# One value buffer instead of two, a twenty-fifth resident weight quarter, and 4 KB output runs in a fused attention and soft-mixture kernel

## The chip, the cores and the metric

The kernel runs on one core of one Trainium2 chip. The metric is the device time of one execution in microseconds (us); what is quoted for a kernel is the median of its runs. A trace is one profiled execution, and its times count from the start of its span.

## What is computed

Forgetting attention over 8 batches of 8 heads, 576 positions and 64 channels, then a soft mixture of 8 experts over all 4608 tokens, in float32 (cut to what matters):

```python
scores = q @ k.T / sqrt(D) + (cum[:, None] - cum[None, :])      # cum = cumsum(log f), causal
attn = softmax(scores); x = (attn @ v) as [4608, 512]           # all heads of a token side by side
logits = x @ phi                                                # 32 slots, 4 for each expert
d = softmax(logits, axis=0); slot_in = d.T @ x                  # over all 4608 tokens: running maximum
slot_out[e] = relu(slot_in[e] @ w1[e]) @ w2[e]                  # w1 [512, 1024], w2 [1024, 512] for each expert
out = softmax(logits, axis=1) @ slot_out
```

The experts need `slot_in` of all tokens, so their two layers and the output can start only when attention has ended. The weights are 33.6 MB, the output 9.4 MB.

## The kernel before, in words

**Attention** works on pairs of heads: 32 pairs, one for each turn of the loop over `g`, with heads `h0 = 2g` and `h1 = 2g + 1`. A turn computes score tiles twice (`s1`, L219, for the row maxima that VectorE takes in `tops`, L232, one and a half pairs ahead; `s2`, L269 and L270, for the exponentials of ScalarE, `expo`, L276), lets GpSimd clear what is above the diagonal (`causal`, L284 and L287), and ends with `s3` (L302): 50 products of the probabilities with the values `V`, on TensorE 100 matmuls in the trace. The order of each engine's instructions is written out by hand; each engine runs its own in that order. `V` holds two pairs: `load_v(g + 1)` (L167) at the head of turn `g` fills the buffer that `s3(g - 1)` has just left, for the turn after.

All loads and stores are issued by SyncE (SP), in order, on one hardware queue that feeds 16 DMA engines. A turn issues, in this order: the values (325 KB), queries and keys of a later pair (`load_qk`, L163, 576 KB), one weight quarter (`wload`, L116, 512 KB) in turns 5 to 28, a row of maxima (L254), and two copies inside SBUF for a later pair (`dup_q` L192 and `dup_k` L188, 288 KB each). These two stand last, so the next turn's `V` queues behind them.

**Weights.** Each expert's two layers are cut into 8 quarters of 512 KB (1024 columns of 128 partitions), 64 in all. 24 (`NRES`) have buffers of their own (`w`) and are loaded during attention. The other 40 are streamed (`wstream`): into buffers that attention leaves (`RAW`, pools `p`, `PTS`, `V`, `XTS`, `X`) from turn 28 on, and at last into the resident buffers as the experts use them up. Quarters are used in the order first layers of all experts, first halves of the second layers, second halves.

**Tail.** After the last turn the last batch's logits give the slot maxima (`spread` L385, `mgroup` L375, `mcast` L398, `tokens` L425, `shift` L440, `shift2` L444, `dispatch` L455), then the slot inputs are turned (L870). `cols` (L683) turns the combine weights of batches n and n + 4 into `cT`. Then come the first layers (`mlp1` L898, ReLU L906 and L908), the turning of their rows into columns (`own` L918, two experts at a time, four times), the second layers (`mlp2` L928) in two halves of the output columns, and the output blocks (`block` L998, copies L1002, stores L1004). While the second halves of the second layers run, blocks of the first half are already computed and stored.

The first 5 (`FIRST`) blocks are done by halves of 256 columns: their stores go out in runs of 1 KB (20 stores of 256 KB). The last 4 blocks are done whole, in runs of 4 KB (8 stores of 512 KB).

Of the kernel before, what the change touches and what calls it, by code (L numbers as in the profile page):

```python
# [18 lines left out]
P = 128  # L19
# [9 lines left out]
NRES = 24  # L29
NQ = 8 * NE  # L30
QW = 1024
FIRST = 5
# [36 lines left out]
def attn_softmoe(ctx: ExitStack, tc: tile.TileContext, qk, v, f, phi, w1, w2, cst, out):  # L69
# [9 lines left out]
    ctok = const.tile([P, B, NBLK, NS], F32, name="ctok")  # L79
# [8 lines left out]
    mask = fr[1].tile([P, 448], F32, name="mask")  # L88
# [13 lines left out]
    V = per.tile([P, 2, NBLK, 130], F32, name="V")  # L102

    LGM = const.tile([P, 290], F32, name="LGM")
    LG, LD, TK = LGM[:, 2:146], LGM[:, 2:162].rearrange("p (t s) -> p t s", t=NBLK), LGM[:, 162:290]
# [59 lines left out]
    def load_v(g):  # L165
        if pair(g):
            nc.sync.dma_start(V[:, g % 2], v[g])  # L167

# [54 lines left out]
    def tops(i, *which):  # L223
        if not head(i):
            return
        g, h = divmod(i, 2)
        for n in which:
            bank, o, blk, j0, w = TOPS[n]
            t = st["top", i % 2, bank]
            m0 = max(448 - (128 * blk + 64) + j0, 0)  # L230
            top = MT[g % 3][:, NBLK * h + blk : NBLK * h + blk + 1] if g else m2[h][:, blk, 1:2]
            nc.vector.tensor_tensor_reduce(  # L232
                out=t[:, o : o + w], in0=t[:, o : o + w], in1=mask[:, m0 : m0 + w], scale=1.0, scalar=top if n == 3 else -3.0e38,
                op0=ALU.add, op1=ALU.max, accum_out=top,
            )
# [61 lines left out]
    def s3(g, values):  # L297

        for h, t, u, c in values:
# [3 lines left out]
                pvv[h][64 * u : 64 * u + 64, t, :], PT[h][:, at : at + 64], V[:, g % 2, c, 65 * h : 65 * h + 65], start=(c == 0), stop=(c == r // 2)  # L303
# [67 lines left out]
    def upper(b):  # L371
        if b < B - 1:
# [45 lines left out]
    def tokens(b, *ns):  # L418
# [5 lines left out]
        for n in ns:  # L424
            nc.tensor.transpose(st["tok", b][:, 128 * n : 128 * n + 128], ((LG if b < B - 1 else V.rearrange("p u t c -> p (u t c)")[:, QW:])[:, 0:128], TK)[n], ident)  # L425

    def tcopy(b):

        if batch(b):
            nc.scalar.copy(ctok[:, b], st["tok", b][:, 0 : NBLK * NS].rearrange("p (t s) -> p t s", t=NBLK))  # L430
# [4 lines left out]
    def shift(b):  # L435
# [4 lines left out]
        nc.vector.tensor_tensor(weight(b), ctok[:, b], top, op=ALU.subtract)  # L440
# [5 lines left out]
    def dispatch(b, *ts):  # L446
# [9 lines left out]
        if NBLK - 1 not in ts:  # L456
            return
# [8 lines left out]
    def combine(b, step):  # L466
# [3 lines left out]
        ce = ctok[:, b]  # L470
# [32 lines left out]
    nc.sync.dma_start(mask, cst[:, 258:706])  # L503
# [134 lines left out]
    load_v(1)  # L638
# [18 lines left out]
    nc.vector.memset(TK, 0.0)  # L657
# [9 lines left out]
    def split(b, *parts):  # L667
# [4 lines left out]
        if 0 in parts:  # L672
            nc.scalar.copy(hi, ctok[:, b::4])
        if 1 in parts:
            nc.vector.tensor_tensor(lo, ctok[:, b::4], hi.bitcast(F32), op=ALU.subtract)
# [17 lines left out]
    for g in range(1, NG):  # L693
# [3 lines left out]
        load_v(g + 1)  # L697
# [69 lines left out]
        tops(u1, 0, 1)  # L767
        s2(h1, 3, 4)
        s1(u1, 4, 5)
        mturn(g + 1)  # L770
        s2(h1, 5)
        mrows(g + 1)
# [7 lines left out]
        if g == 29:  # L780
            sides[2].close()
            p2 = fresh(ctx, "p2", 2)
            wstream(RAW[30 % 3], *p2)
        if g == 30:
# [6 lines left out]
            wstream(*p0, *p1, RAW[31 % 3])  # L791
# [28 lines left out]
        s3(g, VALUES[29:])  # L820
        if w == 0:
# [4 lines left out]
    wstream(V, PTS[:, QW : 2 * QW], PTS[:, 2 * QW : 3 * QW])  # L826
# [19 lines left out]
    srep = PTS[:, 3 * QW : 3 * QW + 128]  # L846
# [12 lines left out]
    dispatch(b - 1, 2, 3, 4)  # L859
# [7 lines left out]
    next(c0)  # L867
    next(c0)
# [6 lines left out]
    for c in (c0, c0, c1, c1, c1, c1):  # L875
        next(c)
# [8 lines left out]
    hs = V.rearrange("p u t c -> p (u t c)")[:, QW : QW + 256], XTS[:, 2 * QW : 2 * QW + 256]  # L885
# [16 lines left out]
    def relu(e):  # L902

        to, scale = hs[e // 2 % 2], mk[:, e : e + 1]
        if e % 2 == 0:
            nc.vector.tensor_scalar(to, PH[e][:, 0:256], scale, 0.0, op0=ALU.mult, op1=ALU.max)  # L906
        else:
            nc.vector.scalar_tensor_tensor(to, in0=PH[e][:, 0:256], scalar=scale, in1=to, op0=ALU.mult, op1=ALU.max)  # L908
# [23 lines left out]

    nc.vector.tensor_scalar_mul(mk, mk, fin[:, 2:3])
# [3 lines left out]
    for e, k in STEPS[:-NE]:  # L937
# [8 lines left out]
        if (e, k) in ((2, 0), (4, 0), (6, 0), (0, 4)):  # L946
            own({2: 0, 4: 2, 6: 4, 0: 6}[e])
# [4 lines left out]
        if (e, k) == (3, 0):  # L952
            combine(b, 1)
            combine(b, 2)
        if (e, k) == (7, 0):
            late.close()
# [8 lines left out]
    outv = out.rearrange("(h m p r) c -> p h m r c", h=2, p=P, r=2)  # L965
    stage = [t.rearrange("p a b -> p (a b)") for t in RAW] + p2 + p0
# [13 lines left out]
    held = [0, 0]  # L980

    def room(w):

        if held[1] + w > QW:
            held[:] = held[0] + 1, 0
        held[1] += w
        return stage[held[0] % len(stage)][:, held[1] - w : held[1]].rearrange("p (r c) -> p r c", r=2)

    def block(m, c=slice(0, DM)):

        w = c.stop - c.start
# [86 lines left out]
```

## Time and profile before

| | |
|---|---|
| median of 3 runs | 385.07 us (384.04 to 386.41) |
| profiled execution | 383.55 us, its span 381.8 us, mean granted TensorE clock 0.987 |
| TensorE (PE) busy | 360.7 us, 94% of the span |
| VectorE (DVE), ScalarE (ACT), GpSimd (POOL) | 74%, 70%, 68% |
| moved by DMA | 93.71 MB, mean 245 GB/s |
| by fortieths of the span, from the 31st on | 156 263 356 366 408 407 406 350 359 337 GB/s |

How to read it: in the first 300 us TensorE is busy nearly all the time and the DMA engines are not; in the last 80 us the DMA engines are full. `PEld` is TensorE's weight load, `SPq` the issue of a DMA by SyncE. A row of a timeline has start, duration, engine, line, operation, output and inputs, count, and in brackets the idle time before it with what ended it.

### The profile page before, as it was taken

How to read it: one execution, taken by the hardware profiler on the slowest of the kernel's cores; microseconds unless marked ns; L12 is line 12 of the kernel's file. 1: busy time of each engine (PE TensorE's matmuls, PEld its weight loads, DVE VectorE, ACT ScalarE, POOL GpSimd, SP SyncE). 2: the span in 40 equal slices, each digit the busy share in tenths (PEclk: the TensorE clock that was granted, in tenths of full speed). 3: DMA queues.
4: the chain of work that ended last, by engine and by line, in shares of the span. 5: the costliest groups of instructions: out<-in, count | busy, mean ns of one | idle time of the engine just before them, and what ended most of it. 6: DMA issues, size and time to landing. Idle time of an engine off the chain costs nothing.

```text
span 381.8 us, 15204 instructions
## 1 busy us (share of the span) xinstructions
PE 360.7 (94%) x5841; PEld 324.6 (85%) x5841; DVE 281.5 (74%) x1134; ACT 268.6 (70%) x673; POOL 261.5 (68%) x377
## 2 busy tenths in 40 slices
PE   7999999999999999999999999999999997999950
PEld 6788999999999999999999999999999985555730
DVE  7987787889788978897889788978888544421551
ACT  8869787878787878787878787878778554002740
POOL 8797888878887888788788888888788832000000
PEclk9999999999999999999999999999999999999995
DMA  7756757677868786878687767777776899999998
GB/s 216 200 154 173 185 162 208 198 230 232 251 182 237 225 252 188 243 211 258 187 244 199 243 199 237 220 217 218 220 217 156 263 356 366 408 407 406 350 359 337
DMA packets 34196, 93.71 MB, mean 245 GB/s; under 512 B 4184, under 2 KB 10126, under 8 KB 34124
## 3 DMA queue, kind: packets, MB, share of 16 engines
q1 hardware_dynamic: 34124, 92.75, 77.7%
q8 instruction: 46, 0.75, 0.8%
q14 instruction: 26, 0.21, 0.2%
HBM read 63.95 MB, written 9.73 MB: 193 GB/s over the span
## 4 chain that ended last, share of the span: by engine, by line
PE 81%; DMA 9%; DVE 3%; ACT 2%; issue 1%; POOL 1%; SPq 0%; DVEq 0%; ACTq 0%; POOLq 0%
PE pv L302 23%; PE ring L269 14%; PE ring L270 12%; PE s L219 12%; PE pv L328 4%; PE ring L898 4%; PE pv L928 2%; PE ds L455 2%; DMA YA<-YA 2%; PE ring L928 2%; PE lg L363 2%; DMA WB<-WA 1%; DMA V<-in_v 1%; DMA V<-in_w 1%; DMA out<-p 1%
## 5 line engine op out<-in xcount | busy, mean ns | idle before, releaser
L276 ACT ACTIVATE PTS<-ring 128x320 f32<-128x320 f32 (+2 forms) x256 | 118.6, 502 | 45.6 <-PE ring L270 41.5
L232 DVE CUSTOM_DVE_ANT_0 s<-s,mask 128x320 f32<-128x320 f32 (+4 forms) x320 | 138.2, 453 | 5.4 <-PE s L219 0.5
L269 PE MATMUL ring<-YA,WA 67*128 67x320 f32 (+9 forms) x384 | 121.6, 329 | 0.6 <-DMA YA<-YA 0.4
L270 PE MATMUL ring<-YB,WB 128*128 128x320 f32 (+4 forms) x384 | 110.7, 296 | 0.0
L302 PE MATMUL pv<-V,PTS 128*64 128x65 f32 x3200 | 102.2, 223 | 1.1 <-POOL PTS L284 1.0
L302 PEld LDWEIGHTS pv<-V,PTS 128*64 128x64 f32 x3200 | 97.1, 138 | 4.2 <-POOL PTS L284 1.5
L219 PE MATMUL s<-WA,YA 66*128 66x288 f32 (+9 forms) x384 | 96.8, 306 | 1.5 <-ACT WA L539 0.4
L198 POOL TENSOR_TENSOR WB<-RAW,WB 64x576 fp32r<-64x576 f32 x64 | 90.4, 1414 | 7.8 <-DMA WB<-WA 2.9
L203 POOL TENSOR_TENSOR YB<-RAW,YA 64x576 fp32r<-64x576 f32 x64 | 89.8, 1422 | 2.5
L269 PEld LDWEIGHTS ring<-YA,WA 67*128 67x128 f32 (+3 forms) x384 | 69.0, 181 | 6.3 <-issue 1.4
L270 PEld LDWEIGHTS ring<-YB,WB 128*128 128x128 f32 (+1 forms) x384 | 69.8, 182 | 0.0
L219 PEld LDWEIGHTS s<-WA,YA 66*128 66x128 f32 (+1 forms) x384 | 64.1, 190 | 5.9 <-DVE LGM L232 1.3
L232 DVE DVE_READ_ACCUMULATOR2_ANT few<- 128x1 f32 x372 | 52.8, 142 | 0.0
L287 POOL TENSOR_SCALAR_AFFINE_SELECT PTS<-PTS 128x128 f32<-128x128 f32 (+1 forms) x128 | 31.5, 267 | 27.4 <-ACT PTS L276 26.3
L172 ACT CAST WA<-RAW 64x576 fp32r<-64x576 f32 x64 | 40.2, 669 | 5.9 <-DMA RAW<-in_qk 5.2
L284 POOL TENSOR_SCALAR_AFFINE_SELECT PTS<-PTS 128x384 f32<-128x384 f32 x64 | 33.4, 523 | 12.5 <-ACT PTS L276 8.1
L177 ACT CAST YA<-RAW 64x576 fp32r<-64x576 f32 x64 | 40.3, 671 | 0.5
L232 DVE CUSTOM_DVE_ANT_0 s<-s,mask,few 128x288 f32<-128x288 f32 x62 | 32.6, 526 | 9.0
L328 PE MATMUL pv<-cs,X 128*128 128x128 f32 x156 | 37.2, 272 | 0.2 <-DVE X L321 0.2
L321 DVE TENSOR_TENSOR X<-pv,rl 128x320 f32<-128x320 f32 (+1 forms) x65 | 31.6, 487 | 2.4 <-DMA V<-in_v 0.3
L316 DVE TENSOR_SCALAR rl<-pv 128x5 f32<-128x5 f32 x64 | 10.5, 164 | 27.8 <-PE pv L302 27.4
L352 ACT COPY XTS<-pv 128x128 f32<-128x128 f32 (+1 forms) x93 | 24.9, 305 | 0.0
(198 smaller groups left out, 345.2 us busy)
## 6 DMA issues: line engine op xcount, KB each, us to landing
w<-in_w SPq DMA_DIRECT2D x45, 512.0 KB
RAW<-in_qk SPq DMA_DIRECT2D x31, 576.0 KB
V<-in_v SPq DMA_DIRECT2D x32, 325.0 KB
WB<-WA SPq DMA_DIRECT2D x31, 288.0 KB
YB<-YA SPq DMA_DIRECT2D x31, 288.0 KB
p<-in_w SPq DMA_DIRECT2D x7, 512.0 KB
out<-RAW SPq DMA_DIRECT2D x12, 256.0 KB
out<-p SPq DMA_DIRECT2D x5, 512.0 KB
```

The costliest lines, as they stand in the source:

```text
L172: nc.scalar.copy(WA[g % 3][0:64, S * h : S * h + S], RAW[g % 3][64:128, h])
L177: nc.scalar.copy(YA[g % 3][0:64, h, 64:640], RAW[g % 3][0:64, h])
L198: nc.gpsimd.tensor_tensor(t[0:64], RAW[g % 3][64:128, h], t[64:128].bitcast(F32), op=ALU.subtract)
L203: nc.gpsimd.tensor_tensor(YB[g % 2][64:128, h], RAW[g % 3][0:64, h], YA[g % 3][0:64, h, 64:640].bitcast(F32), op=ALU.subtract)
L219: nc.tensor.matmul(t[:, o : o + w], ya[0:m, h, 128 * blk : 128 * blk + 128], wa[0:m, j0 : j0 + w], start=True, stop=True)
L232: nc.vector.tensor_tensor_reduce(out=t[:, o : o + w], in0=t[:, o : o + w], in1=mask[:, m0 : m0 + w], scale=1.0, scalar=top if n == 3 else ...
L269: nc.tensor.matmul(o, wa[0:m, j0 : j0 + n], ya[0:m, h, 64 + i0 : 64 + i0 + w], start=True, stop=False)
L270: nc.tensor.matmul(o, wb[:, j0 : j0 + n], yb[:, h, i0 : i0 + w], start=False, stop=True)
L276: nc.scalar.activation(PT[i % 2][:, SEG_O[bank] : SEG_O[bank] + at], t[:, 0:at], AF.Exp, scale=0.125)
L284: nc.gpsimd.affine_select(d3, d3, pattern=[[0, 3], [1, 128]], compare_op=ALU.is_ge, fill=0.0, base=0, channel_multiplier=-1)
L302: nc.tensor.matmul(pvv[h][64 * u : 64 * u + 64, t, :], PT[h][:, at : at + 64], V[:, g % 2, c, 65 * h : 65 * h + 65], start=(c == 0), stop= ...
L328: nc.tensor.transpose(pm[:, 0:128], x[:, t, p % 2, 0:128], ident)
```

## The change

It does these things at once:

- `V` has one buffer. `load_v(g)` takes the place of `load_v(g + 1)` at the head of turn `g`; the values of pairs 30 and 31 are loaded at the end of turns 29 and 30, behind `s3`.
- The room (with a shorter mask whose zeros are read twice, `ctok` for 7 batches, and `TK` laid into `PTS`) makes a 25th resident quarter, loaded in turn 29. 39 quarters are streamed.
- The last batch: `mgroup` before `spread`, `spread` on three engines from a copy in `VF`, three steps of `dispatch(6)` ahead of `mcast`.
- `own` turns all experts' rows once, after the last first layer, with `cols` of batches 2, 6 and 3, 7 on either side of it.
- The output is laid out as [2, 9, 128, 1024], so that each half block is one store of 512 KB in 4 KB runs: 18 stores. The rows are put in order outside the device program.

```diff
-NRES = 24
+NRES = 25
-FIRST = 5
...
-    V = per.tile([P, 2, NBLK, 130], F32, name="V")
+    V = per.tile([P, NBLK, 130], F32, name="V")
+    VF = V.rearrange("p t c -> p (t c)")
...
     def load_v(g):
         if pair(g):
-            nc.sync.dma_start(V[:, g % 2], v[g])
+            nc.sync.dma_start(V, v[g])
...
+            if m0 < 0:
+                to = to.rearrange("p (a c) -> p a c", a=2)
+                by = mask[:, 0 : w // 2].rearrange("p (o c) -> p o c", o=1).broadcast_to([P, 2, w // 2])
...
-        load_v(g + 1)
+        if g < NG - 2:
+            load_v(g)
...
             p2 = fresh(ctx, "p2", 2)
-            wstream(RAW[30 % 3], *p2)
...
-            wstream(*p0, *p1, RAW[31 % 3])
+            wstream(*p0, *p1[:2])
...
         s3(g, VALUES[29:])
+        if g in (29, 30):
+            load_v(g + 1)
+            wstream(*((RAW[0], *p2) if g == 29 else (p1[2], RAW[1])))
...
     wstream(XTS[:, 0:QW])
+    mgroup(b)
     spread(b)
-    mgroup(b)
-    dispatch(b - 1, 1)
+    dispatch(b - 1, 1, 2, 3)
     mcast(b)
...
-    def own(e):
-        pm = turn()
+    def own():
+        pm = po[1]
         for c in range(2):
-            nc.tensor.transpose(pm[:, 128 * c : 128 * c + 128], hs[e // 2 % 2][:, 128 * c : 128 * c + 128], ident)
-        for n in (e, e + 1):
+            nc.tensor.transpose(pm[:, 128 * c : 128 * c + 128], hs[:, 128 * c : 128 * c + 128], ident)
+        for n in range(NE):
...
-        if (e, k) in ((2, 0), (4, 0), (6, 0), (0, 4)):
-            own({2: 0, 4: 2, 6: 4, 0: 6}[e])
...
         if (e, k) == (7, 0):
+            for _ in c2:
+                pass
+            own()
+            for _ in c3:
+                pass
...
+    def block(m, c):
+        stage.append(stage.pop(0))
+        o, pm = stage[-1], [turn() for _ in range(2)]
         for r in range(2):
...
+        for h in range(2):
+            copies[h](o[:, 512 * h : 512 * h + 512], pm[h])
+        nc.sync.dma_start(out[c, m], o)
...
     ring += [bank[0], po[0]]
-    block(0, half[0])
-    block(1, half[0])
+    block(0, 0)
     mlp2(3, 1)
+    block(1, 0)
     mlp2(4, 1)
-    block(2, half[0])
     mlp2(5, 1)
+    block(2, 0)
     mlp2(6, 1)
...
     mlp2(7, 1)
     gathered(1)
-    block(4, half[0])
+    block(3, 0)
+    block(4, 0)
```

What the diff does not tell is how the queues stand now. On SP, at the end of attention (turns 29 to 31; `RAW`, `p`, `PTS` and `w` here are weight quarters, `YA` the row of maxima, `YB` and `WB` the two copies), before:

```order
L167 DMA V<-in_v 128x650
L254 DMA YA_87<-YA_83 1x10x128
L192 DMA YB_85<-YA_83 64x2x576
L188 DMA WB_86<-WA_84 64x1152
L116 DMA RAW_93<-in_w 128x1024
L116 DMA p_0_5290<-in_w 128x1024
L116 DMA p_1_5291<-in_w 128x1024
L167 DMA V<-in_v 128x650
L254 DMA YA_83<-YA_83 1x10x128
L116 DMA p_0_5438<-in_w 128x1024
L116 DMA p_0_5442<-in_w 128x1024
L116 DMA p_1_5443<-in_w 128x1024
```

and now:

```order
L167 DMA V<-in_v 128x650
L116 DMA w_128<-in_w 128x1024
...
L192 DMA YB_85<-YA_83 64x2x576
L188 DMA WB_86<-WA_84 64x1152
L167 DMA V<-in_v 128x650
L116 DMA RAW_93<-in_w 128x1024
...
L260 DMA YA_83<-YA_83 1x10x128
L116 DMA p_0_5438<-in_w 128x1024
L116 DMA p_0_5442<-in_w 128x1024
L116 DMA p_1_5443<-in_w 128x1024
L167 DMA V<-in_v 128x650
L116 DMA p_2_5444<-in_w 128x1024
```

The first `V` row is pair 30 before and pair 29 now; the last `V` row is pair 31 in both. Before, it stood ahead of the first quarters into `p_0_5438` and its two neighbours; now it stands behind all three.

On TensorE, the last batch's chain before (L455 is `dispatch(6)` into `ring`, and `dispatch(7)` into `more`):

```order
L363 MATMUL lg_5568<-XTS,phis 32x144 x4
L455 MATMUL ring_139<-X_97,LGM 32x129 x2
L455 MATMUL ring_139<-X_98,LGM 32x129 x2
L398 MATMUL pv_138<-cs,mb_5678 128x128
L425 MATMUL more_5647<-cs,V 128x128
L425 MATMUL more_5647<-cs,LGM 128x128
```

and now, all of it up to the same place:

```order
L369 MATMUL lg_5569<-XTS,phis 32x144 x4
L467 MATMUL ring_140<-X_97,LGM 32x129 x2
L467 MATMUL ring_140<-X_98,LGM 32x129 x2
...
L407 MATMUL pv_139<-cs,mb_5676 128x128
L434 MATMUL more_5649<-cs,V 128x128
L434 MATMUL more_5649<-cs,PTS 128x128
```

The pair of L467 rows stands three times in a row now, the pair of L455 rows stood once: the broadcast of the maxima (L407, before L398) follows three steps of `dispatch(6)` instead of one.

On TensorE between the first and the second layers, now:

```order
L922 MATMUL ring_142<-p_1_5443,LGM 32x256 x4
L698 MATMUL more_5650<-cs,cw_5830 128x128 x2
L698 MATMUL pv_139<-cs,cw_5830 128x128 x2
L698 MATMUL pv_139<-cs,cw_5830 128x64
L942 MATMUL pv_138<-cs,V 128x128 x2
L698 MATMUL lg_5569<-cs,cw_5882 128x128 x2
L698 MATMUL more_5649<-cs,cw_5882 128x128 x2
L698 MATMUL more_5649<-cs,cw_5882 128x64
L952 MATMUL ring_140<-p_2_5444,X_97 32x256 x4
```

The two sets of L698 (`cols`) stood among the second halves of the second layers and behind them before, and the L942 row (`own`) stood four times, three of them between first layers.

## Rows read from the trace of the kernel before

**Rows 1.** The page, shares of the chain that ended last, by engine
```profile
PE 81%; DMA 9%; DVE 3%; ACT 2%; issue 1%; POOL 1%; SPq 0%; DVEq 0%; ACTq 0%; POOLq 0%
```

**Rows 2.** Windows: us, busy (count) PE, PEld, DVE, ACT, POOL; clock, DMA share, GB/s
```profile
323.00:353.00 30.00, 30.00 (x497) 17.05 (x498) 8.57 (x28) 3.20 (x10) 0.00 (x0) 1.00 1.03 408
...
364.00:370.00 6.00, 4.00 (x23) 1.89 (x20) 2.83 (x5) 2.78 (x5) 0.00 (x0) 1.00 1.04 351
372.00:380.00 8.00, 0.00 (x0) 0.00 (x0) 1.29 (x2) 1.07 (x2) 0.00 (x0) 0.50 1.02 405
```

**Rows 3.** Timeline of SP in the tail: streamed quarters, then first stores
```profile
323.71 22.77 SPq L116 DMA_DIRECT2D w<-in_w  x21
350.47 5.04 SPq L1004 DMA_DIRECT2D out<-RAW  x6
```

**Rows 4.** Timeline of SP: issues of values, and what stands beside them
```profile
27.00 0.84 SPq L167 DMA_DIRECT2D V<-in_v  x1
27.93 1.42 SPq L163 DMA_DIRECT2D RAW<-in_qk  x1
...
55.02 0.51 SPq L167 DMA_DIRECT2D V<-in_v  x1
...
288.29 1.47 SPq L167 DMA_DIRECT2D V<-in_v  x1
...
304.58 3.55 SPq L116 DMA_DIRECT2D p<-in_w  x4
```

**Rows 5.** Timeline of PE: `s3` of turns 1, 4, 29 and 31
```profile
31.43 1.50 PE L302 MATMUL pv<-V,PTS 128*64 128x65 f32 x42
33.62 1.96 PE L302 MATMUL pv<-V,PTS 128*64 128x65 f32 x58 [0.70 <-POOL PTS L284]
...
59.26 3.14 PE L302 MATMUL pv<-V,PTS 128*64 128x65 f32 x100
...
294.38 3.14 PE L302 MATMUL pv<-V,PTS 128*64 128x65 f32 x100
...
310.77 3.19 PE L302 MATMUL pv<-V,PTS 128*64 128x65 f32 x100
```

**Rows 6.** Windows around three loads of values, columns as in rows 2
```profile
27.00:32.40 5.40, 5.40 (x67) 4.93 (x67) 4.97 (x22) 5.26 (x14) 4.08 (x6) 1.00 1.00 269
287.00:293.50 6.50, 6.50 (x85) 6.07 (x81) 5.22 (x23) 5.43 (x15) 5.50 (x11) 1.00 0.87 221
305.60:310.40 4.80, 4.45 (x40) 3.69 (x37) 1.78 (x6) 3.02 (x10) 1.89 (x6) 1.00 0.96 327
```

**Rows 7.** Timeline of ACT: the keys that queue behind the values of 27.00
```profile
34.50 1.24 ACT L172 CAST WA<-RAW 64x576 fp32r<-64x576 f32 x2 [0.68 <-DMA RAW<-in_qk]
```

**Rows 8.** The chain of waits, start and us: values from issue to landing
```profile
300.12 5.34 DMA V<-in_v
```

**Rows 9.** Timeline of ACT, DVE and PE: the last batch's maxima
```profile
316.76 0.75 ACT L385 COPY LGM<-lg 32x32 f32<-32x32 f32 x4 [0.88 <-PE lg L363]
317.54 0.37 DVE L375 CUSTOM_DVE_ANT_0 V<-lg,few,LGM 128x144 f32<-128x144 f32 x1 [1.36 <-ACT LGM L385]
317.98 0.32 PE L398 MATMUL pv<-cs,mb 128*128 128x128 f32 x1 [1.06 <-DVE mb L375]
318.45 0.87 PE L455 MATMUL ring<-X,LGM 128*32 128x129 f32 x24
```

**Rows 10.** Timeline of PE: `cols`, second layers' second halves; DVE: a copy
```profile
322.22 0.86 PE L683 MATMUL more<-cs,cw 128*128 128x128 f32 x5
...
345.78 1.05 PE L928 MATMUL pv<-w,X 128*32 128x256 f32 x16
347.38 1.93 PE L928 MATMUL pv<-w,X 128*32 128x256 f32 x32
350.75 1.07 PE L928 MATMUL pv<-w,X 128*32 128x256 f32 x16
...
369.93 0.69 DVE L1002 COPY p<-ring 128x512 f32<-128x512 f32 x1 [1.58 <-DMA out<-p]
```

More of the change, by code (lines that the diff above doesn't have):

```diff
@@ L455, in dispatch, with gather @@
                 nc.tensor.matmul(ds[32 * j : 32 * j + 32, 0:129], weight(b)[:, t, :], x, start=(t == 0), stop=(t == NBLK - 1))
-        if NBLK - 1 not in ts:
-            return
+        if NBLK - 1 in ts and b != B - 2:
+            gather(b)
+    def gather(b):
+        ds = st["ds"]
         if b == 0:
@@ L469, in combine @@
             return
-        ce = ctok[:, b]
+        ce = tokenwise(b)
         if step == 0:
@@ L672, in split @@
         if 0 in parts:
-            nc.scalar.copy(hi, ctok[:, b::4])
+            for n in range(2):
+                nc.scalar.copy(hi[:, n], tokenwise(b + 4 * n))
         if 1 in parts:
-            nc.vector.tensor_tensor(lo, ctok[:, b::4], hi.bitcast(F32), op=ALU.subtract)
+            for n in range(2):
+                nc.vector.tensor_tensor(lo[:, n], tokenwise(b + 4 * n), hi[:, n].bitcast(F32), op=ALU.subtract)
     def cols(b, bank):
@@ L858, in attn_softmoe @@
     mine(b)
-    dispatch(b - 1, 2, 3, 4)
+    dispatch(b - 1, 4)
+    gather(b - 1)
     wstream(X[0], X[1])
@@ L866, in attn_softmoe @@
     ps = turn()
-    next(c0)
-    next(c0)
+    for _ in c0:
+        pass
     slT = LD.rearrange("p t s -> p (t s)")[:, 0:128]
@@ L931, in mlp2 @@
                 )
+    c2, c3 = (cols(n, turn) for n in (2, 3))
     nc.vector.tensor_scalar_mul(mk, mk, fin[:, 2:3])
@@ L964, in attn_softmoe @@
     NT = B * S // (4 * P)
-    outv = out.rearrange("(h m p r) c -> p h m r c", h=2, p=P, r=2)
-    stage = [t.rearrange("p a b -> p (a b)") for t in RAW] + p2 + p0
+    stage = [t.rearrange("p a b -> p (a b)")[:, 0:QW] for t in RAW] + p2 + p0
     copies = [nc.scalar.copy, nc.vector.tensor_copy]
@@ L978, in halve @@
         nc.vector.tensor_tensor(SO[1][:, half[n]], pr[n], SO[0][:, half[n]].bitcast(F32), op=ALU.subtract)
[L980 to L991, printed above, removed]
-        o = [room(2 * w) for _ in range(2)]
+    def block(m, c):
+        stage.append(stage.pop(0))
+        o, pm = stage[-1], [turn() for _ in range(2)]
         for r in range(2):
-            pm = [turn()[:, 0:w] for _ in range(2)]
+            at = 256 * m + 128 * r
             for part in range(2):
@@ L998, in block @@
                     nc.tensor.matmul(
-                        pm[h], cT[rows, 256 * m + r : 256 * m + 256 : 2], SO[part][rows, c], start=(part == 0), stop=(part == 1)
+                        pm[h][:, 256 * r : 256 * r + 256], cT[rows, at : at + 128], SO[part][rows, half[c]], start=(part == 0), stop=(part == 1)
                     )
-            for h in range(2):
-                copies[h](o[h][:, r], pm[h])
         for h in range(2):
-            nc.sync.dma_start(outv[:, h, m, :, c], o[h])
-    c2, c3 = (cols(n, turn) for n in (2, 3))
+            copies[h](o[:, 512 * h : 512 * h + 512], pm[h])
+        nc.sync.dma_start(out[c, m], o)
     gathered(0)
@@ L1013, in attn_softmoe @@
     ring += [bank[0], po[0]]
-    block(0, half[0])
-    block(1, half[0])
+    block(0, 0)
     mlp2(3, 1)
+    block(1, 0)
     mlp2(4, 1)
-    block(2, half[0])
     mlp2(5, 1)
+    block(2, 0)
     mlp2(6, 1)
-    for _ in c2:
-        pass
-    split(3, 0, 1)
-    block(3, half[0])
     mlp2(7, 1)
     gathered(1)
-    block(4, half[0])
+    block(3, 0)
+    block(4, 0)
     slots(1)
     halve(1)
-    for _ in c3:
-        pass
     ring += [bank[1], po[1]]
-    for m in range(FIRST):
-        block(m, half[1])
-    for m in range(FIRST, NT):
-        block(m)
+    for c, m in [(0, m) for m in range(5, NT)] + [(1, m) for m in range(NT)]:
+        block(m, c)
 def kernel(q, k, v, f, moe_phi, moe_w1, moe_w2):
```

71 lines of the change are left out of this document (43 added, 28 removed).

## The prediction

> **What bounds the kernel now.** I read the chain of waits first, then the windows of the tail, then SP's queue, then TensorE's rows where it meets that queue. TensorE stands on 81% of the chain [rows 1]: through attention, whatever makes TensorE wait is added to the time, since no later turn has slack to give it back. In the tail two things run full together: between 323 and 353 us TensorE is busy without a gap and the DMA engines are full at 408 GB/s [rows 2]. So the tail pays for bytes, and also for the moment at which TensorE has the first output blocks ready. The last streamed quarters are issued up to 346.5 us, the first store at 350.47 [rows 3]: stores queue behind quarters, and when the quarters have landed, the stores alone decide.
>
> The change gives to the tail and takes from attention. I cost it in five terms against the profiled execution, whose span is 381.8 us.
>
> **1. One value buffer.** The load's issue does not move: it waits for the end of the same `s3` as before. What moves is its deadline, a whole turn nearer: the values issued at the head of a turn are now needed by that turn's own `s3`. No row of before shows this wait, so I bound it turn by turn from issue, traffic and the start of `s3`.
>
> Turn 1: issued at 27.00, `s3` starts at 31.43 [rows 4, 5]. In front of the load stand two copies of 288 KB, behind it queries and keys of 576 KB. The window 27.0 to 32.4 is full at 269 GB/s, 1.45 MB [rows 6], and the copies and values together are 0.92 MB, done after 3.4 us at that rate: 30.4 is the earliest landing. The load queued behind is used at 34.50 after a wait [rows 7]: the latest. From issue, another load of values with a full queue in front took 5.34 us [rows 8], the keys behind this one 6.5; I take 5.9 us between them, so 32.9. That is 1.5 us late. But 0.70 us of it is already paid: this `s3` stops later for GpSimd [rows 5], and that stop goes when the start is late. Net **+0.8** (0 to 2.3).
>
> Turns 2 to 28: in a short turn the issue is at 55.02 and `s3` at 59.26, 4.2 us [rows 4, 5]. By the traffic alone 3.4 us are needed plus some tenths to land. I take **0**; if the 5.34 us held there, each such turn (one in four) would lose 1.1 us. Kept for the range: 0 to 7.
>
> Turn 29: issued at 288.29 behind the two copies and one streamed quarter, 1.45 MB in all, and the window 287.0 to 293.5 moved 1.44 MB [rows 6]; a landing at about 294.9 if the slowest of the 16 engines runs 1 us behind the mean, against `s3` at 294.38 [rows 5]: **+0.5** (0 to 1.0).
>
> Turn 30: the values now lead their queue, ahead of the quarters. I cost it at nothing: the score work of that turn hides it, and without that cover it would cost as turn 1 does.
>
> Turn 31: the load stands behind three streamed quarters issued from 304.58 [rows 4]. These are 1.57 MB, just what the window 305.6 to 310.4 moved [rows 6]. The values' 0.33 MB end 0.8 us later, 311.2, and land about 311.7; `s3` started at 310.77 [rows 5]: **+0.9** (0 to 1.3).
>
> Together **+2.2** (0 to 8).
>
> **2. The last batch's maxima.** Before, VectorE idled 1.36 us until ScalarE's four copies were out, and the broadcast on TensorE idled 1.06 us for VectorE [rows 9]. Now VectorE can start 0.75 us earlier. But three steps of `dispatch` now stand before the broadcast: 24 such matmuls take 0.87 us [rows 9], from about 316.7 to 317.55, against 317.98 before. So 0.4 us are won, not 0.75; the copies of `spread`, now behind, take some 0.4 us on three engines and end about when TensorE gets there. **-0.4** (-0.75 to +0.5, if they end last).
>
> **3. Turning.** Two sets of `cols`, 0.86 us each [rows 10], move ahead of the second layers: +1.7. Three of the four turnings of expert rows go; each is two transposes, at the pace of `cols` 0.35 us: -1.05. ReLU of the last expert (about half a microsecond) hides under the first `cols`, the eight small copies under the second `cols` and the first second layers. **+0.6** until the second halves start (0 to +1.2, if a copy or cast is waited for).
>
> **4. The output.** Before, from the start of the second halves, 345.78 [rows 10], to the span's end are 36.0 us. Now, from that same start: two experts take about 1.9 us [rows 10], so eight take 7.5; a half block, two of which fit between 349.31 and 350.75 [rows 10], takes 0.72. The fourth half block is computed after all eight experts, one small product and three blocks: 7.5 + 0.6 + 4 x 0.72 = 11.0 us. Its copy is 0.69 [rows 10], and from issue to first bytes of a store I estimate 1.1 (the three quarters of 304.58 moved from 305.6 [rows 4, 6]). So its bytes start at +12.8 us, and from there 15 stores of 0.524 MB at 405 GB/s follow without a gap: 19.4 us; then 1.4 us to the span's end (the engines were full past 380 [rows 2], and the span ended at 381.8). 33.6, that is **-2.4**. The first three half blocks are not enough to fill the DMA engines until then: about 2 us stay idle there. Without this hole the gain would be the bytes alone: 5.24 MB at 351 GB/s before and 405 now [rows 2], 14.9 to 12.9 us, and less dips that 1 KB runs had beside it, up to -3.3. With one more hole of the same size it is -0.8.
>
> Here a rule speaks against the change. The Trainium skill (DMA: Bandwidth & Descriptors, Why small descriptors are slow) counts a fixed 3 bus cycles for a packet of size/32; by that, 1 KB runs pay 9% and 4 KB runs 2%, and as an estimate from that page the bytes would win 0.9 us, not 2.0. The rows say 15%, with the engines full in both stretches; they decide.
>
> **5. The 25th quarter.** One quarter less is streamed, 1.3 us of full DMA. But values of a whole pair now travel in the full stretch too, 0.33 MB, 0.8 us, so the streamed quarters end 0.5 us earlier relative to TensorE. By term 4 TensorE, not the quarters, sets the fourth block: **0** here (0 to -0.5). The quarter moved into turn 29 lies in the idle DMA time behind the values, and nothing waits for it.
>
> Costed at nothing: the mask read in two pieces (VectorE's element counts stay), `TK` in `PTS` (written by GpSimd after `s3` has read that place, read before the odd head's exponentials), the split casts of `ctok`. VectorE has a quarter of its time free to cover them; without it they would cost some hundredths in a head.
>
> **Sum**: 2.2 - 0.4 + 0.6 - 2.4 + 0 = 0.0 us. The profiled execution took 383.55, 1.5 below the median of 385.07; put on the median the forecast is **385.0 us**, no change.
>
> **Rivals.**
>
> *Values hidden after all.* If loads land as early as traffic alone allows, term 1 is 0.3 and the tail keeps its gain, with the bytes at -2.9: 0.3 - 0.4 + 0.6 - 2.9 - 0.3 = -2.7, **382.4**. For it: the earliest bounds of turns 1 and 29. Against: the keys behind the first load come at 34.50, far later than traffic alone allows.
>
> *Values late in every short turn* (slower). TensorE stops at the head of `s3` in turns like that of 59.26. It decides once issue to landing passes 4.2 us, and one load was seen to take 5.34, though behind three quarters. Seven turns at 0.6 us: +4.2, so **389.2**. It would be worse in long turns only past 5 us.
>
> *Runs are not the matter.* The 351 GB/s of the stretch with 1 KB runs could come from something else there, such as stores issued too late, and stay. Then term 4 loses its 2.0 us of bytes and keeps 0.4: +2.0, **387.0**. Against it: the DMA share of that window is 1.04, not below one [rows 2]. The Trainium skill (DMA: Bandwidth & Descriptors, Specifications) names 512 B as the size from which a transfer runs at line rate, which would make this case the likely one.
>
> *The tail without a hole and more.* If ScalarE and VectorE hand over blocks sooner and the streamed quarters end earlier, DMA alone decides from their end, terms 2 and 3 drop out, and with term 1 near 0.3 it is 0.3 - 3.3 - 0.5 = -3.5, **381.6**.
>
> **Chances.** Forecast 0.50, values hidden 0.20, values late 0.14, runs not the matter 0.09, tail without a hole 0.07. One per cent, 3.85 us, is about what a measurement of this kernel can tell from no change; so faster means below 381.2, slower above 388.9. The forecast's own range is 383 to 387. With the rivals to either side the range is **381.4 to 388.6**. Faster 0.10 (half of the last case, a third of the first rival), same 0.77, slower 0.13 (over half of the late case, the upper ends of the others).
>
> **What would show it.** Right: TensorE's rows at `s3` of turns 1, 29 and 31 carry idle time that ended by a DMA of `V`, 0.5 to 1.5 us each, and those of turns 2 to 28 almost none; the first layers start 1 to 2 us later than 323; all stores run at about 405 GB/s; between the third and fourth store the DMA share dips for about a microsecond. Wrong: waits for `V` in many turns (late), none at all (hidden), stores of 4 KB runs near 350 GB/s (runs not the matter), or a tail in which the stores follow the quarters with no dip.

## The result, and the profile after

| | before | after |
|---|---|---|
| median (range) | 384.43 us (383.2 to 387.17) | 387.51 us (386.03 to 389.38), 14 runs each |
| ratio | | 1.0074 (95%: 1.0054 to 1.0093) |
| profiled execution, its span | 383.55 us, 381.8 us | 386.76 us, 385.0 us |

The change made the kernel 0.7% slower: 3.1 us in the medians, 3.2 us in the spans, where the sum of the terms had been 0.0. (The median of before is that of the 14 runs beside those of after. Every row below is of one profiled execution of its kernel, and its time can lie a microsecond or two from the kernel's median.)

The place is in the chain of waits of the changed kernel (start us, us, what), around `s3` of turn 31, now L308:

```profile
306.93 7.90 DMA V<-in_v
314.83 0.04 issue
314.87 4.60 PE pv L308 x80
319.48 0.87 PE lg L369 x24
```

The values of pair 31 were issued at 306.93 and landed 7.90 us later. `s3` started at 314.87 instead of 310.77 [rows 5], 4.10 us late, and then it also took 4.60 us instead of 3.19. Its end, at 319.48, is 5.5 us late. The windows of the changed kernel (columns as in rows 2) show why `s3` was slow, and what the transfers did meanwhile:

```profile
305.60:310.40 4.80, 4.36 (x43) 3.60 (x39) 1.90 (x6) 2.95 (x9) 1.85 (x6) 1.00 0.80 262
...
312.00:314.00 2.00, 0.00 (x0) 0.00 (x0) 1.01 (x4) 1.08 (x5) 0.53 (x3) 1.00 0.97 360
314.00:316.00 2.00, 1.13 (x20) 1.13 (x22) 0.00 (x0) 0.00 (x0) 0.00 (x0) 0.67 1.00 405
316.00:318.00 2.00, 2.00 (x43) 2.00 (x42) 0.00 (x0) 0.00 (x0) 0.00 (x0) 0.50 0.36 141
318.00:320.00 2.00, 2.00 (x68) 1.93 (x68) 1.23 (x6) 0.00 (x0) 0.00 (x0) 0.98 0.35 78
323.00:353.00 30.00, 29.12 (x496) 17.64 (x499) 10.61 (x41) 6.38 (x20) 2.14 (x8) 1.00 1.02 398
364.00:370.00 6.00, 5.28 (x74) 4.77 (x70) 4.42 (x8) 3.66 (x8) 0.00 (x0) 1.00 1.01 404
372.00:380.00 8.00, 0.58 (x8) 0.38 (x7) 2.77 (x4) 2.34 (x4) 0.00 (x0) 0.76 1.02 405
```

Look at the granted clock, third from the right. TensorE does nothing from 312 to 314; then the clock falls from 1.00 to 0.50 (1.2 GHz), and `s3` runs through 316 to 318 at that level. Look at the last column next. The window 305.6 to 310.4 moved 262 GB/s, where it was 327 [rows 6]. From 316 to 320 the transfers nearly stopped (141 and 78 GB/s): the next quarters go into `PTS`, which `s3` must have read, and SP waited 7.0 us for `s3` (L308) before it issued them at 318.38. SP's timeline shows both places:

```profile
304.55 2.28 SPq L116 DMA_DIRECT2D p<-in_w  x3
306.93 0.38 SPq L167 DMA_DIRECT2D V<-in_v  x1
...
318.38 1.50 SPq L116 DMA_DIRECT2D PTS<-in_w  x3
...
328.44 22.48 SPq L116 DMA_DIRECT2D w<-in_w  x21
```

From there the delay moves into the tail. TensorE's timeline, `s3` of turns 1 and 29, last logits, broadcast, first layers, second halves:

```profile
32.65 3.53 PE L308 MATMUL pv<-V,PTS 128*64 128x65 f32 x100 [1.12 <-DMA V<-in_v]
...
294.35 3.14 PE L308 MATMUL pv<-V,PTS 128*64 128x65 f32 x100
...
321.80 0.45 PE L369 MATMUL lg<-XTS,phis 128*32 128x144 f32 x8 [0.31 <-DVE XTS L343]
322.85 0.32 PE L407 MATMUL pv<-cs,mb 128*128 128x128 f32 x1
327.74 1.50 PE L922 MATMUL ring<-w,LGM 128*32 128x256 f32 x24
...
350.42 1.05 PE L952 MATMUL pv<-w,X 128*32 128x256 f32 x16
...
360.59 0.64 PE L952 MATMUL pv<-w,XTS 128*32 128x256 f32 x8 [0.33 <-DMA w<-in_w]
```

For comparison, the same points before (`lg` L363, first layers L898):

```profile
316.24 0.45 PE L363 MATMUL lg<-XTS,phis 128*32 128x144 f32 x8 [0.31 <-DVE XTS L337]
...
323.01 5.39 PE L898 MATMUL ring<-w,LGM 128*32 128x256 f32 x96
```

The lag of after behind before is 5.56 us at the last logits (321.80 against 316.24), 4.73 at the first layers (327.74 against 323.01), 4.64 at the second halves (350.42 against 345.78 [rows 10]) and 3.2 at the end of the span. So in these two executions all of the loss is made at one `s3`; the last batch gives back 0.83, the turning 0.09, the output 1.4.

### The profile page after: what moved, and what is told of

Its sections match the earlier page's. It is cut to its first block, busy times and chain, and to the rows that moved or that the text cites. A ratio compares the mean times of both kernels' runs of the same rounds, so it can differ in the third digit from the quotient of the medians.

```text
span 385.0 us, 15222 instructions
## 1 busy us (share of the span) xinstructions
PE 360.0 (93%) x5867; PEld 326.2 (85%) x5867; DVE 280.8 (73%) x1128; ACT 269.3 (70%) x665; POOL 261.6 (68%) x378
## 4 chain that ended last, share of the span: by engine, by line
PE 81%; DMA 12%; DVE 2%; ACT 2%; issue 1%; POOL 1%; SPq 0%; ACTq 0%; DVEq 0%; POOLq 0%
PE pv L308 24%; PE ring L275 14%; PE s L219 12%; PE ring L276 12%; PE pv L334 4%; PE ring L922 4%; DMA w<-in_w 3%; PE lg L369 2%; DMA out<-p 2%; DMA V<-in_v 2%; PE ds L467 2%; PE ring L952 2%; DMA WB<-WA 1%; DMA YA<-YA 1%; DMA out<-RAW 1%
## 5 line engine op out<-in xcount | busy, mean ns | idle before, releaser
L308 PE MATMUL pv<-V,PTS 128*64 128x65 f32 x3200 | 103.0, 224 | 5.1 <-DMA V<-in_v 5.0
L308 PEld LDWEIGHTS pv<-V,PTS 128*64 128x64 f32 x3200 | 98.2, 139 | 8.1 <-DMA V<-in_v 5.2
L238 DVE CUSTOM_DVE_ANT_0 s<-s,mask 128x320 f32<-128x320 f32 (+2 forms) x192 | 71.7, 375 | 4.4
L238 DVE CUSTOM_DVE_ANT_1 s<-s,mask 128x288 f32<-128x288 f32 (+1 forms) x128 | 72.7, 568 | 0.7
```

What stands on the lines that cost most here:

```text
L238: nc.vector.tensor_tensor_reduce(out=to, in0=to, in1=by, scale=1.0, scalar=top if n == 3 else -3.0e38, op0=ALU.add, op1=ALU.max, accum_out ...
L308: nc.tensor.matmul(pvv[h][64 * u : 64 * u + 64, t, :], PT[h][:, at : at + 64], V[:, c, 65 * h : 65 * h + 65], start=(c == 0), stop=(c == r ...
```

## The experiments

Unless said otherwise an edit is made to the changed kernel. Ratios are to the kernel before, with 95% intervals.

**Is it the place of the load in its queue?** In turn 30 the three quarters go behind the values:

```diff
-            wstream(*p0, *p1[:2])
...
-            wstream(*((RAW[0], *p2) if g == 29 else (p1[2], RAW[1])))
+            wstream(*((RAW[0], *p2) if g == 29 else (*p0, *p1, RAW[1])))
```

> The changed kernel with the values of pair 31 first in their queue: the three weight quarters that stood ahead of them in turn 30 are issued behind them. Theory (the values of pair 31 come late because they stand behind three quarters; TensorE idles 3.9 us for them and then runs s3 at half the granted clock): the load lands 3 to 3.5 us after its issue like that of turn 30 (298.04 to 301.35), about 310.2, so the wait is below 0.5 us, s3 takes 3.2 us instead of 4.60, and ends near 314.5 instead of 319.48. The quarters start 2.3 us later, but the transfers no longer run dry at 318 to 319.3, so of the 5 us only some 1.5 to 2.5 reach the end: 385.0 to 386.0. Rival A (it is not the place in the queue but slow traffic in that stretch): the wait stays above 2 us and the time at 387.5. Rival B (the loss lies in the tail, in the turning and the order of the last batch): s3 ends 5 us earlier and the time stays at 387.5 within 0.5.

Measured: **384.05 us, 0.9985 (0.9968 to 1.0001)**. No wait at `s3`, which takes 3.19 us. The theory holds and both rivals fall; the gain on the changed kernel, 3.5 us in the medians, is more than expected.

**Is that place enough by itself?** The kernel before, with both its value buffers; the load of pair 31 goes where the changed kernel has it, and the last two quarters of that turn go behind it:

```diff
-        load_v(g + 1)
+        if g != 30:
+            load_v(g + 1)
...
-            wstream(*p0, *p1, RAW[31 % 3])
+            wstream(*p0, *p1[:2])
...
         s3(g, VALUES[29:])
+        if g == 30:
+            load_v(g + 1)
+            wstream(p1[2], RAW[1])
```

> The kernel before, all its buffers kept, with nothing changed but the place of the load of pair 31's values: from the head of turn 30 to the end of that turn, behind three weight quarters, where the changed kernel has it. Theory (this place alone makes the loss): TensorE waits 2.5 to 4.5 us at s3 of turn 31, the granted clock falls if the wait is long, the transfers run low behind it, and the time rises by 2 to 4 us: 386.5 to 388.5. Rival (the wait also needs the single buffer or the changed streams of turns 29 and 30): within 0.7 of before, 384.4 to 385.4.

Measured: **388.7 us, 1.0095 (1.0064 to 1.0126)**. This one edit makes a loss as large as the whole change (1.0074; the intervals overlap), though the wait in the profile is 1.67 us, shorter than the 2.5 to 4.5 expected. TensorE's row of `s3`, and two windows behind it:

```profile
313.36 4.70 PE L302 MATMUL pv<-V,PTS 128*64 128x65 f32 x100 [1.67 <-DMA V<-in_v]
```

```profile
314.00:316.00 2.00, 2.00 (x42) 2.00 (x40) 0.04 (x1) 0.00 (x0) 0.00 (x0) 0.50 0.91 367
316.00:318.00 2.00, 2.00 (x59) 1.93 (x56) 0.85 (x3) 0.00 (x0) 0.00 (x0) 0.80 0.15 29
```

A wait of 1.67 us is followed by the same clock of 0.50, the same long `s3` and the same gap in the transfers.

**Values early, in a place of their own.** Pair 31's values go into a buffer of `p1`, issued at 305.51 ahead of the quarters; the quarter of that buffer comes only after `s3` (main lines; `VS` lists the value buffers, and `s3` of turn 31 reads the last):

```diff
+            VS.append(p1[2][:, 0 : NBLK * 130].rearrange("p (t c) -> p t c", t=NBLK))
+            load_v(g + 1)
             wstream(*p0, *p1[:2])
...
-    wstream(PTS[:, QW : 2 * QW], PTS[:, 2 * QW : 3 * QW])
+    wstream(p1[2], PTS[:, QW : 2 * QW], PTS[:, 2 * QW : 3 * QW])
```

> The changed kernel with the values of pair 31 in a place of their own (the third buffer of the pool p1, which takes its weight quarter only after s3 of turn 31), loaded at 304.6, ahead of the quarters, which keep their issue. Theory: no wait for these values at all, s3 of turn 31 starts at 310.8 and takes 3.2 us at the full granted clock, ends at 314.0 (before 313.96), and the transfers go on without running dry: 2.5 to 4 us less than the changed kernel, 383.5 to 385.0. Rival A (slow traffic): a wait of over 1 us in spite of the early load. Rival B (the loss lies in the tail): no wait, and yet 387 or more.

Measured: **385.33 us, 1.0022 (1.0005 to 1.0039)**, 0.3 above the range of the theory: the wait is gone (`s3` starts at 311.87 and takes 3.19 us), and most of the loss with it. What is left may lie in its transfers, which have a quarter less in the queue and are slow in these windows, but that was only read, not tried:

```profile
306.00:308.00 2.00, 2.00 (x44) 1.88 (x38) 1.58 (x7) 0.21 (x1) 1.40 (x3) 1.00 0.65 181
...
318.00:320.00 2.00, 1.48 (x30) 0.68 (x19) 1.13 (x8) 0.75 (x4) 0.53 (x3) 1.00 0.89 291
```

**Two value buffers and 24 resident quarters, the rest of the change kept** (main lines).

```diff
-NRES = 25
+NRES = 24
...
-            nc.sync.dma_start(V, v[g])
+            nc.sync.dma_start(V[:, g % 2], v[g])
...
-        if g < NG - 2:
-            load_v(g)
+        load_v(g + 1)
```

> The changed kernel with two value buffers, loaded a turn ahead as before, and 24 resident quarters; the short mask, the order of the last batch, the turning in one go and the output in 4 KB runs stay. Theory (the single buffer and where it puts the load of pair 31 are the whole loss, the other parts together gain): no wait for values, s3 of turn 31 ends near 314, the span of the last batch from there to the first layers stays 0.8 us shorter than before: 382.5 to 384.0, below the 384.4 of before. Rival (the turning in one go or the order of the last batch costs in the tail): 385 or more.

Measured: **384.64 us, 0.9993 (0.9967 to 1.002)**. Not the gain expected, and not the rival's 385.

**The output.** First alone, on the kernel before (layout, `block` and copies of the changed kernel; only its store is shown), then the changed kernel with runs of 1 KB:

```diff
-        for h in range(2):
-            nc.sync.dma_start(outv[:, h, m, :, c], o[h])
+        nc.sync.dma_start(out[c, m], o)
```

```diff
-        nc.sync.dma_start(out[c, m], o)
+        nc.sync.dma_start(out[m, :, :, c], o.rearrange("p (r c) -> p r c", r=4))
```

> The kernel before with the output part of the change alone: 18 stores of half blocks in 4 KB runs, the copies by halves; two value buffers, 24 resident quarters, the last batch and the turnings as before. Theory (the tail's gain is that of the output, and the loss is that of the values): 2.4 us less than before, between 0.8 and 3.3: 382.0. Rival (the output gains little, and what the changed kernel gives back in its tail comes from the 25th quarter and the turning): within 0.5 of before, 384.4.

> The changed kernel with its 18 stores in the same order and of the same size, but written in runs of 1 KB, into a layout of [9, 128, 4, 2, 256]. Theory (the runs are worth 15% of the rate, 351 against 405 GB/s): 18 stores of 0.524 MB take 1.49 us each instead of 1.29; those that follow one another at the end, about 15, cost 3.0 us more: 390.5, between 389.7 and 391.2. Rival (runs are not the matter; the rate came from the order of the stores or from what ran beside them): 387.5 within 0.6.

Measured: output alone **382.97 us, 0.9965 (0.9951 to 0.998)**, a gain in the range expected, 1 us short of its middle. Runs of 1 KB: **391.25 us, 1.0172 (1.0143 to 1.0201)**, 3.7 us more than the changed kernel and at the upper end of what was expected. Two windows of the run with 1 KB, with the DMA engines full or nearly so, stand against 404 and 405 GB/s of after:

```profile
364.00:370.00 6.00, 5.12 (x78) 4.70 (x74) 4.37 (x8) 3.53 (x8) 0.00 (x0) 1.00 0.94 314
372.00:380.00 8.00, 2.59 (x16) 2.00 (x16) 3.46 (x5) 2.93 (x5) 0.00 (x0) 0.50 1.03 343
```

405 against 343 is 18%. The Trainium skill (Perfetto Trace Analysis, DMA Optimizations) advises larger transfers because those below 2 KB carry a significant overhead each. It speaks of whole transfers, and these stores are 512 KB either way; read for their runs, the rows agree with it, and not with the 9% against 2% of the rule weighed in the prediction.

**The hole before the fourth store.** With the values first, blocks 3 and 4 go ahead of the last two experts:

```diff
+    block(3, 0)
     mlp2(6, 1)
+    block(4, 0)
     mlp2(7, 1)
     gathered(1)
-    block(3, 0)
-    block(4, 0)
```

> The run with the values of pair 31 first in their queue, and the fourth and fifth half block moved ahead of the last two experts' second halves, where TensorE waits for weights (0.59 and 0.62 us in that run). Theory (the fourth store comes too late, and the hole of about 1 us in the transfers at 360 is on the path): the hole goes and the time falls by 0.7 to 1.2 us: 383.0, below before by 0.3 to 0.5%. Rival (the hole is made up behind by transfers that would wait anyway): the same within 0.3.

Measured: **383.3 us, 0.9961 (0.9939 to 0.9983)**. The hole is gone (the window 359 to 361 moves 223 GB/s with the values first alone, 389 here). The ratio falls from 0.9985 to 0.9961, some 0.9 us, as expected, but the two intervals overlap. The same blocks with two value buffers:

> Two value buffers and 24 resident quarters with the other parts of the change, and the fourth and fifth half block early. Theory (that run lost its gain of the output to the hole of a microsecond that the later blocks make): 0.7 to 1.0 us less than without the early blocks, 383.8, level with the output part alone on the kernel before (0.9965). Rival (the turning or the last batch costs something): 384.6 as without.

Measured: **383.48 us, 0.9976 (0.9953 to 0.9999)**, against 0.9993 without the early blocks, some 0.7 us, the intervals again overlapping.

**How many quarters may stand ahead?** With the blocks early, one, two and three quarters are issued ahead of the values; for one:

```diff
-            wstream(*p0, *p1[:2])
+            wstream(*p0)
...
-            wstream(*((RAW[0], *p2) if g == 29 else (p1[2], RAW[1])))
+            wstream(*((RAW[0], *p2) if g == 29 else (*p1, RAW[1])))
```

> The run with the values of pair 31 first and the fourth and fifth half block early, but with one weight quarter (p0) issued ahead of these values, at 304.6, instead of none. Theory (the values need only to be early enough; the transfers stood nearly still from 306 to 308, at 27 GB/s, for want of anything in the queue): the quarter is through by about 307.6, the values of issue 306.9 land by 310.5, ahead of s3 at 311, no wait; the streamed quarters come 1 to 1.3 us earlier than with none ahead, and so does the end: 382.2 (381.6 to 383.0), 0.993 of before. Rival (TensorE, not the transfers, sets the end now): the same as with none ahead, 383.3.

> The same with two quarters ahead of the values of pair 31. Quarters in this stretch took 1.3 to 2.1 us each in the runs so far. Theory: the values land between 310.3 and 311.6, against s3 at about 311.0: a wait of 0 to 0.6 us, no fall of the granted clock, and 382.2 to 383.2. Rival (it is slow traffic, whatever stands ahead): a wait of over 1.5 us as with three, 385 or more.

> The changed kernel (three quarters ahead of the values of pair 31) with the fourth and fifth half block moved ahead of the last two experts' second halves. Theory: the wait for the values stays as in the changed kernel, 1 to 4 us with a fall of the clock where it is long; the hole between third and fourth store goes, 0.7 to 1.0 us: 386.7. It closes the series of none, one, two and three quarters ahead, all with the blocks early. Rival (the hole costs nothing where the quarters are late anyway): 387.5.

| quarters ahead | wait at `s3` | `s3` | median | ratio |
|---|---|---|---|---|
| none | none | 3.19 us | 383.3 us | 0.9961 (0.9939 to 0.9983) |
| one | none | 3.19 | 382.88 | 0.9945 (0.992 to 0.997) |
| two | 1.99 us | 4.71 | 384.08 | 0.9989 (0.9964 to 1.0013) |
| three | 2.74 | 4.71 | 388.1 | 1.0082 (1.0051 to 1.0113) |

Waits and `s3` are those of the profiled execution. TensorE's rows of one, two and three:

```profile
313.41 3.19 PE L308 MATMUL pv<-V,PTS 128*64 128x65 f32 x100
```

```profile
314.09 4.71 PE L308 MATMUL pv<-V,PTS 128*64 128x65 f32 x100 [1.99 <-DMA V<-in_v]
```

```profile
316.60 4.71 PE L308 MATMUL pv<-V,PTS 128*64 128x65 f32 x100 [2.74 <-DMA V<-in_v]
```

The wait in the profile grows with the number of quarters ahead. In time three is clearly told apart from the others, two from one barely (0.0044, give or take 0.0035), none from one not. Two were expected to do; they cost 1.99 us of waiting in the profile, and the runs spread from 381.59 to 386.73, so the margin is gone. With one ahead it is small: the last packet of the values starts at 312.89, 0.5 us before `s3`. The early blocks gain nothing with three ahead, as the rival had it. One ahead has the lowest ratio of this study, but that of the output alone (0.9965) lies within its interval.

**What part has the clock?** First the changed kernel with work for TensorE while it waits:

```diff
+        if g == NG - 1:
+            warm(12, cs)
         s3(g, VALUES[:29])
```

> The changed kernel with 12 idle products (128x184, into a free bank, 24 matmuls) on TensorE ahead of s3 of turn 31, about 3.7 us of work in the time in which it waits for the values of pair 31. Theory (s3 of turn 31 takes 4.60 us instead of 3.19 because the granted clock fell to 0.50 after 3.9 us of idling): s3 starts when the values land, as before, at about 314.9, but runs at a granted clock of 1.00 in 3.2 us and ends at 318.1 instead of 319.48; what follows comes 1.3 us earlier, and so does the end, since the transfers that ran dry wait for s3: 386.2 (385.8 to 387.0). Rival (s3 is long because its values and probabilities come in late or because transfers disturb it): s3 takes 4.6 us again at a clock of 1.00, and the time is 387.5.

Measured: 387.58 us, 1.0071 (1.0047 to 1.0094). The rows have the short `s3` of the theory, the time is the rival's:

```profile
310.81 3.99 PE L507 MATMUL pv<-cs 128*128 128x184 f32 x24
314.73 3.14 PE L308 MATMUL pv<-V,PTS 128*64 128x65 f32 x100
```

It doesn't tell, since the wait differs between executions (1.24 us in the profile of the run with 1 KB, whose program is the same up to there), and where it is short the added work is itself a delay. So a fixed delay went into the kernel with the values first and the blocks early, once with TensorE busy (the same 12 products), once idle (VectorE takes the maximum of the values with themselves after the last scores; the second idle run has four such operations, the first had five, behind other work of the turn):

```diff
+            nc.vector.tensor_copy(small.tile([P, 1], F32, name="seen"), st["bank"][0][:, 0:1])
+            for _ in range(4):
+                nc.vector.tensor_tensor(VF, VF, VF, op=ALU.max)
```

> The run with the values of pair 31 first and the blocks early (383.3), in which no wait for values is left, with a delay put ahead of s3 of turn 31 on purpose: 12 idle products on TensorE, 4.0 us, so that TensorE is late but never idle. Theory (a late s3 holds back the three quarters that go into PTS, the transfers run dry for part of the delay, and the clock comes on top where TensorE idles): s3 takes 3.2 us at a granted clock of 1.00; the quarters issued before last until about 316, so some 2 to 2.8 us of the 4.0 reach the end: 385.3 to 386.1. Rival (the end is set by the transfers alone and has room): 383.3 to 384.3. Rival (all of the delay passes through): 387.3.

> The same delay with TensorE idle: s3 of turn 31 waits for five operations of VectorE on the values, which leave them as they are and start when the last scores are done, about 3.8 to 4.2 us. Theory (the fall of the granted clock behind the idling is a part of the loss of its own): s3 takes 4.6 us at 0.50, ends 1.4 us later than in the run with the same delay and TensorE busy, and the time is 1.0 to 1.6 us longer than there: 386.5 to 387.5. Rival (the clock falls, but what it costs is hidden): within 0.5 of the busy run.

> The delay with TensorE idle once more, with its length mended: in the run before it VectorE's operations stood behind others of the turn, and TensorE idled 6.69 us instead of 4. Now four of them stand first, from the end of the last scores: s3 of turn 31 should start at about 315.4, as in the busy run (315.44). Theory (the fall of the clock passes to the end): s3 takes 4.7 us instead of 3.14, and the time is 1.0 to 1.6 us above the busy run, 388.2, ratio to before 1.009 to 1.011 against 1.0061. Rival (the clock's part is hidden): ratio 1.0061 within 0.002.

Measured: busy **386.91 us, 1.0061 (1.0044 to 1.0079)**; idle for 6.69 us, too long to compare, 391.34 us, 1.0176 (1.0146 to 1.0206); idle for 4.72 us **389.34 us, 1.0147 (1.0127 to 1.0168)**, more than the 1.009 to 1.011 expected; `s3` started at 316.95 instead of about 315.4. TensorE's rows of the busy run, then of the run that idles 4.72 us, and a window of that:

```profile
311.52 3.99 PE L507 MATMUL pv<-cs 128*128 128x184 f32 x24
315.44 3.14 PE L308 MATMUL pv<-V,PTS 128*64 128x65 f32 x100
```

```profile
316.95 5.68 PE L308 MATMUL pv<-V,PTS 128*64 128x65 f32 x100 [4.72 <-DVE V L832]
```

```profile
318.00:322.00 4.00, 4.00 (x80) 4.00 (x79) 0.85 (x3) 0.00 (x0) 0.00 (x0) 0.50 0.17 45
```

Behind the idling `s3` takes 5.68 us at 0.50, not 3.14, and ends at 322.6 instead of 318.6. Of these 4.0 us, 1.5 are a later start and 2.5 the clock; the time differs by 0.0086 of 384.1, 3.3 us, give or take 1.0. Even if all of the later start passed through, some 1.8 us would be left for the clock: its part reaches the end. The idle run also delays VectorE, but that adds nothing up to the last logits: they come 4.06 us later than in the busy run (324.96 against 320.90), as `s3`'s end does. The busy run's own delay (`s3` ends 3.75 us later than without) costs 0.0100, 3.8 us give or take 1.1, as the second rival had it; the spans of the two profiled executions differ by less, 2.8 us.

## Why the prediction was wrong, point by point

**Term 1, turn 31, is the step that failed.** It put +0.9 (0 to 1.3): "the load stands behind three streamed quarters", 1.57 MB, "just what the window 305.6 to 310.4 moved", landing at 311.7. The wait was foreseen; its price was not, in two ways.

- The landing was taken from bytes over the rate of one window of another program. That window moved 262 GB/s here, and the values came at 314.83. A measured latency for the same case stood in the rows, 5.34 us behind three quarters [rows 8], and was used for turn 1 but not here; from the issue seen here, 306.93, it gives 312.3, above the upper end. Even that is too little: 7.90 was measured. The range should have started from it. The packets in the trace (2,600 B each for values, 4,096 B for quarters) show why bytes ahead are not enough: the values' packets start between 310.2 and 314.3, and some 160 packets of quarters issued behind them start before the last one. With the load alone moved, in the kernel before, they start between 310.7 and 312.7.
- That a wait makes the work behind it slower was not priced at all: 1.4 us in `s3` (4.60 against 3.19) at the granted clock of 0.50. The Trainium skill (TensorE: Matmul & The Clock Gate, HAM oscillation — how this bites in real kernels) describes such a case in another kernel, a wait for a transfer that lets the clock fall so that the work behind it starts slow; the delays, busy and idle, agree (an `s3` of 3.14 and 5.68 us).

Together 5.5 us where 0.9 stood.

**The rest of term 1.** Turn 1: a wait of 1.12 us where 1.5 were expected, and the stop for GpSimd went; `s3` ends at 36.18 instead of 35.58, +0.6 against +0.8. So the wait was sized well, but it is not added to the time. The prediction held that no later turn would give it back; turn 2 did. Before, its `s3` stopped for GpSimd as well; that stop went too, and this `s3` ends at 44.83 instead of 45.05. Turn 2, before and after:

```profile
41.26 1.50 PE L302 MATMUL pv<-V,PTS 128*64 128x65 f32 x42
43.09 1.96 PE L302 MATMUL pv<-V,PTS 128*64 128x65 f32 x58 [0.34 <-POOL PTS L284]
```

```profile
41.69 3.14 PE L308 MATMUL pv<-V,PTS 128*64 128x65 f32 x100
```

Turns 2 to 28 at 0: right in this execution; in three other profiles with one value buffer (values first, values first with the blocks early, idle for 4.72 us) turn 28 waits 0.6 to 0.7 us for values. Here all idle time ahead of `s3` that ended by values is 5.0 us, the waits of turns 1 and 31:

```profile
L308 PE MATMUL pv<-V,PTS 128*64 128x65 f32 x3200 | 103.0, 224 | 5.1 <-DMA V<-in_v 5.0
```

Turn 29 was put at +0.5; it has no wait (294.35 against 294.38). Turn 30 at nothing: right.

**Terms 2 and 3**, -0.4 and +0.6. From the last logits to the first layers 5.94 us instead of 6.77, -0.8; from there to the second halves 22.68 instead of 22.77, -0.1. The maxima gained twice what was put, the turning cost nothing.

**Term 4**, -2.4 (-3.3 to -0.8). From the start of the second halves to the span's end 34.6 instead of 36.0 us: -1.4. That runs matter was right, and shown (18% of the rate, 3.7 us). The hole was there, 211 GB/s in the window 362 to 364. What was wrong is the statement that TensorE, not the quarters, sets the fourth block: TensorE waited 0.33 us for weights at 360.59, a third of the missing 1.0. The quarters were late with attention: the last streamed ones were issued up to 350.92, where it was 346.48 before.

**Term 5**, 0: the 25th quarter was not tried by itself, so this stays open.

**The sum** of these: +5.56 - 0.83 - 0.09 - 1.44 = +3.2 us, the difference of the spans. Of the rivals, "runs are not the matter" came nearest in time (387.0), by luck: the run with 1 KB refutes it. Values late in every short turn (389.2) was wrong in kind: one turn, not seven.

**Open.** Why the stretch before 312 moved 262 GB/s here and 327 and 324 in the kernel before and in the run with the output alone, and why the values' packets are spread so wide in it. The loss does not need the slow stretch: with the load moved alone in the kernel before, the window 308 to 312 moved 387 GB/s (274 in the changed kernel), and the wait and the slow `s3` came all the same. Also why two value buffers with the rest of the change (0.9976 with the early blocks) aren't better than the output alone (0.9965): the intervals overlap.

## What to carry to other kernels

Price a load by the longest issue-to-landing time that the trace has for the same position in the queue, not by bytes over a rate, and take that as the least: behind three quarters it was 5.34 us in the kernel before, and 6.26, 7.28 and 7.90 in three profiles with one value buffer. A wait of some microseconds in a busy TensorE has a second price, the slow work behind it, and perhaps a third where transfers wait for buffers that this work must leave, which was not measured by itself. When a buffer is given up, move the load of its last user to the front of its queue: here this moves the ratio from 1.0074 to 0.9985. With the blocks early it is 0.9961, and with one quarter ahead 0.9945; neither of these two steps is clear of the noise by itself.

## What had not been expected of the hardware

Ahead of `s3` of turn 31 the granted clock fell to 0.50 with idle times of TensorE of 1.67, 1.99, 2.74, 3.90, 4.72 and 6.69 us, each time with an `s3` of 4.60 us or more. Below that it went both ways. The run with 1 KB has two waits of 1.24 us in one execution, at turn 1 and at turn 31: the clock fell at the first and stayed at the second. At turn 1 of the run with two quarters ahead it stayed behind 1.37 us. The rows of the run with 1 KB and a window behind its first wait, then the row of two ahead:

```profile
32.73 4.71 PE L308 MATMUL pv<-V,PTS 128*64 128x65 f32 x100 [1.24 <-DMA V<-in_v]
...
315.47 3.14 PE L308 MATMUL pv<-V,PTS 128*64 128x65 f32 x100 [1.24 <-DMA V<-in_v]
```

```profile
34.00:36.00 2.00, 2.00 (x43) 2.00 (x42) 0.00 (x0) 1.83 (x4) 1.92 (x4) 0.50 0.07 16
```

```profile
32.88 3.14 PE L308 MATMUL pv<-V,PTS 128*64 128x65 f32 x100 [1.37 <-DMA V<-in_v]
```

So among waits this short the length of the wait does not settle whether the work behind it runs slow; what does, these runs don't show.
